# A retention-and-Mish kernel whose first q loads are cut into four pieces, with the order of its opening changed

## The chip, the cores and the metric

The kernel runs on one core of one Trainium2 chip. The metric is the device time of one launch in microseconds (us). A profile of one further execution shows what each engine did: PE (matrix products; PEld is its weight load), DVE (vector), ACT (activation), POOL (GpSimd) and SP, which issues the DMAs.

## The reference

A decaying linear attention is followed by a feed-forward layer with the activation Mish, for 4 batches, 8 heads, 768 positions, head size 64, and an inner width of 2048:

```python
for t in range(S):
    state = gamma * state + outer(k[:, :, t], v[:, :, t])
    y[:, :, t] = scale * einsum(q[:, :, t], state)
x = y.transpose(0, 2, 1, 3).reshape(B * S, H * D)      # 3072 x 512
h = x @ w_in                                           # 512 x 2048
out = (h * tanh(softplus(h))) @ w_out                  # 2048 x 512
```

Everything is float32 in memory; the kernel multiplies in float16.

## The kernel before, in words

**Tiling.** The recurrence is done in chunks of 128 positions. Within a chunk, scores q k^T are masked and multiplied with v; a state of 64 x 64 per head carries what came earlier. The decay is put into the casts: q and k are multiplied with tables of powers of gamma while they are cast from float32 to float16. The 24 chunks form blocks: the first block has four chunks (512 positions, handled as two pairs of chunks), the others two. A block's y, turned so that features lie on the partitions, is `xts[blk]`; `g1` multiplies it with w_in and applies Mish, and the output functions multiply with w_out. Sums of products are saved in places by combining halves (`first_sums`, `weight_sums`: `s1` to `s4`, `t1` to `t4`).

**Order.** It is written by hand: each engine runs its instructions in the order in which the program issues them. All loads go through SP's queue. Load buffers rotate; the float32 stage for q of the first block and for the weights (`wt`, four buffers) is shared.

**The opening** (`first_block`, L1219). SP issues q of the first 512 positions in two halves of four heads (`load_first_q`, L244), then k and v of both pairs in halves of four heads (`load_pair`, L289), 256 KB each; I write k(0,1) for pair 0, second half. Then come the weights (`load_weights`, L1195): w_in in four slices of 512 columns, win0 in four loads, win1 and win2 in two each, by even and odd row blocks, win3 in one, and then slices of w_out. PE fills its waits with `spin` (L454), products of the identity whose results nobody reads.

For each half of q and k there is a cast (`turn_first_q`, L269, and `cast_pair`, L292; on DVE, or POOL where nothing else is said), transposes on PE (`turn_parts`, L253) and a copy from PSUM to SBUF (`taken`, L263; ACT or DVE). Then:

- `pair_scores(n, a)` (L332): 16 products of turned k and q for half a of pair n, and a mask on DVE (L349).
- `cast_pair(n, "v", a)`: v is scaled on ACT (L307).
- `pair_outer` (L356): outer products k^T v, for the state; `pair_state` (L368) adds them up: `mid` on ACT for the first chunk (L373), `suh` and `sth` on DVE (L378, L380), `mid` on DVE for pair 1 (L375).
- `pair_present` (L383): masked scores times v, in two parts; between them PE waits for a copy of one element, `seen` (L1269 on ACT, L1276 on DVE), which shows that the first part is done.
- `pair_past` (L395): the state times q. `pair_xt` (L405) casts the finished y into `xts[0]`.

**Behind the opening.** `open_in` (L671) multiplies `xts[0]` with win0 in an order that follows what is ready (L682). The later units of the first block are `g1(0, u)`, u = 4 to 15, each four products of 128 x 512 with one 128-column part of win1, win2 and win3 (L711) and one Mish on ACT (L720). `first_out` (L756) is the output of the first block; its products are L768. The product of `s3` and `t3` needs L862, a DVE subtraction of parts of wout2 and wout0.

Of the kernel before, what the change touches and what calls it, by code (L numbers as in the profile page):

```python
# [9 lines left out]
FP16 = mybir.dt.float16  # L10
FP32 = mybir.dt.float32
# [5 lines left out]
def kernel(  # L17
# [9 lines left out]
    nc = tc.nc  # L27
# [213 lines left out]

    def load_first_q():  # L244

        qf = wstage.tile([P, H, CPB, D], FP32, name="qfirst", tag="wt", bufs=4)
        for a in range(0, H, H // 2):
            nc.sync.dma_start(
                qf[:, a:a + H // 2],
                q[0, a:a + H // 2, :TB].rearrange("h (p r) d -> p h r d", r=CPB))  # L250
        return qf

    def turn_parts(parts, dst, on_act=False):  # L253
        t_ps = mmps.tile(list(dst.shape), FP16, name="t_ps", tag="mm")
        turn_only(parts, t_ps)
        taken(dst, t_ps, on_act)
# [9 lines left out]
        else:  # L266
            nc.vector.tensor_copy(dst, t_ps)

    def turn_first_q(qf, a, on_act, between=None):  # L269
        n = H // 2  # L270
        q16 = castp.tile([P, 2 * CPB, 2, D], FP16, name="qk16", bufs=4)
        mine = slice(a * n, (a + 1) * n)
        nc.vector.tensor_tensor(  # L273
            in_place(q16), by_head(qf[:, mine]), scale_by_head(qs_four[:, mine]), op=ALU.mult)
        if between is not None:
            between()
        qt = qktp.tile([P, HP // 2, CPB, P], FP16, name="qkt", bufs=6)
        turn_parts(lambda i, r: q16[:, i * CPB + r], qt, on_act)
        first_q.append(qt)

    first_q, pairs = [], {}

    def room_pair(n, names="kv"):
        pairs[n] = {
# [4 lines left out]
    def load_pair(n, nm, a, queue):  # L289
        queue.dma_start(pairs[n][nm][a], pair_src({"q": q, "k": k, "v": v}[nm], n, a))  # L290
# [380 lines left out]
    def open_in():  # L671
# [21 lines left out]
        for f in range(FPS):  # L693
# [3 lines left out]
            if f < 2:  # L697
                nc.scalar.activation(gts[0, f], h[f], AF.Mish, scale=inv_boost3)
        nc.scalar.activation(gtiles[0, 0][:, 2:FPS], two, AF.Mish, scale=inv_boost3)

    def g1(blk, u):
        nt = BLOCKS[blk] * C
# [514 lines left out]
            load_one(g, 2, nc.sync)  # L1217

    def first_block():  # L1219
        qf = load_first_q()  # L1220
        for n in range(2):
            room_pair(n)
        for nm in "kv":
            for n in range(2):
                for a in range(2):
                    load_pair(n, nm, a, nc.sync)
        load_weights()

        pair_at(0, 0)
        spin(46, 1)  # L1230
        turn_first_q(qf, 0, True)
        spin(14, 2)
        turn_first_q(qf, 1, False, lambda: cast_pair(0, "k", 0, vs_two, nc.vector))
        for n, a in ((0, 1), (1, 0), (1, 1)):
            cast_pair(n, "k", a, vs_two)
        nc.gpsimd.memset(tri_half, 0.0)
        for n in range(2):
            nc.gpsimd.affine_select(
                out=tri_half[half(n)], in_=tri_half[half(n)], compare_op=ALU.is_gt, fill=1.0,
                base=0, pattern=[[-1, 2], [-2, D // 2]], channel_multiplier=1)  # L1240
        keep_from(keep_two, 2, [[1, 2], [-1, 2], [-2, D]])
        turn_pair(0, "k", 0, True)
        spin(14)
        pair_scores(0, 0)
        pair_at(0, 1)
        turn_pair(0, "k", 1, True)
        spin(14)
        pair_scores(0, 1)
        turn_pair(1, "k", 0, True)
        cast_pair(0, "v", 0)  # L1250
        turn_pair(1, "k", 1, True)
        cast_pair(0, "v", 1)
        cast_pair(1, "v", 0)
        pair_at(1, 0)
        spin(8)
        pair_scores(1, 0)
        u = [mmps.tile([P, HP, D], FP32, name="u_ps", tag="mm") for _ in range(2)]
        pair_outer(0, u, 0)
        pair_at(1, 1)
        spin(4)  # L1260
        pair_scores(1, 1)
        pair_outer(0, u, 1)
        pair_state(0, u, 0)
        y = [pool.tile([P, 2, 2, C], FP32, name="y_ps", tag=tag)
             for pool, tag in ((mmps, "mm"), (pxps, "px"))]
# [54 lines left out]
        for u in range(NFB):  # L1320
            if u == 0:
                open_in()
            elif u >= FPS:
                g1(0, u)
            if u == 2 * FPS + FPS - 1:
                sums, make = first_sums()
                make[0]()
                make[1]()
                cast_wout(0)
                sum_weights(0, 1)  # L1330
                make[2]()
                cast_wout(1)
                make[3]()
                cast_wout(2)
# [209 lines left out]
```

## Time and profile before

| | |
|---|---|
| median of 3 runs | 191.63 us (191.41 to 191.92) |
| the profiled execution | 191.53 us |
| its span, first to last instruction | 189.7 us |
| PE / DVE / ACT / POOL busy | 97% / 76% / 55% / 39% of the span |
| DMA | 38.82 MB, mean 205 GB/s |

A row of the timeline gives the start in us from the span's start, the time that it covers, the engine, the source line, the operation with what it writes and reads, the shape, the count, and in brackets how long the engine sat idle before it and what ended that. Rows of one kind that follow each other are merged. A product's end is modelled and overlaps the next, so starts are what to compare. DMA rows give the size and the median time from issue to landing. In rows of stages, each engine has its busy time and, in brackets, its count of instructions; the last three columns are the granted PE clock, the share of the 16 DMA engines and the rate.

### The profile page before, as it was taken

To read this page: it belongs to the slowest core of one execution; us is meant where nothing else is said; L and a number is where in the kernel's file an instruction comes from. 1 tells how busy PE (TensorE), PEld (TensorE's weight loads), DVE (VectorE), ACT (ScalarE), POOL (GpSimd) and SP (SyncE) were. 2 spreads that over 40 slices of the span, in tenths; PEclk is the share of its full clock that TensorE was granted. 3 is DMA by queue.
4 is the path that set the end of the run, shared out by engine and by line. 5 is a ranking of instruction groups with operands and counts; after the bars stand their busy time and mean duration, and the time that the engine had idled before them with its cause. 6 is when DMAs were issued, how large, how long until landed. Compare 5 with 4: busy or idle time off the path is not lost.

```text
span 189.7 us, 7650 instructions
## 1 busy us (share of the span) xinstructions
PE 184.5 (97%) x3310; PEld 162.3 (86%) x3310; DVE 144.1 (76%) x297; ACT 105.2 (55%) x199; POOL 73.2 (39%) x101
## 2 busy tenths in 40 slices
PE   7999999999999999999999999999999999999993
PEld 7656478888888888888998998998998998988983
DVE  0788649895977978997898597696698698666862
ACT  3365766264643552553584584583683773873651
POOL 5273000578409746941564624714534800000000
PEclk9999999999999999999999999999999999999999
DMA  5999999999999999999999968992899980301103
GB/s 166 307 314 386 387 384 366 301 315 218 148 249 322 169 235 227 157 276 222 231 211 279 159 143 173 234 206 43 195 198 239 213 162 3 116 3 49 65 3 112
DMA packets 83234, 38.82 MB, mean 205 GB/s; under 512 B 58240, under 2 KB 76288, under 8 KB 83200
## 3 DMA queue, kind: packets, MB, share of 16 engines
q1 hardware_dynamic: 82912, 38.22, 86.3%
q8 instruction: 26, 0.43, 1.1%
q10 hardware_dynamic: 288, 0.11, 0.3%
q14 instruction: 8, 0.07, 0.2%
HBM read 27.31 MB, written 6.29 MB: 177 GB/s over the span
## 4 chain that ended last, share of the span: by engine, by line
PE 94%; DMA 2%; DVE 1%; ACT 1%; issue 0%; DVEq 0%
PE h_ps L923 23%; PE o_ps L1109 23%; PE h_ps L711 17%; PE o_ps L1013 10%; PE o_ps L768 7%; PE y_ps L603 3%; DMA qfirst<-in_q_dram 2%; PE h_ps L682 2%; PE t_ps L261 2%; PE u_ps L497 1%; PE at L489 1%; PE at L460 1%; PE y_ps L390 1%; PE at L341 1%; DVE qk L273 1%; PE u_ps L362 0%
## 5 line engine op out<-in xcount | busy, mean ns | idle before, releaser
L711 PE MATMUL h_ps<-xt,win 128*128 128x256 f16 (+1 forms) x268 | 32.6, 281 | 0.0
L711 PEld LDWEIGHTS <-win 128*128 128x128 f16 x268 | 26.0, 98 | 5.4 <-DVE win L221 0.2
L720 ACT ACTIVATE g<-h_ps 128x512 f16<-128x512 f32 x36 | 21.5, 597 | 14.7 <-PE h_ps L711 14.7
L923 PE MATMUL h_ps<-xt,wsum 128*128 128x128 f16 x448 | 29.6, 219 | 0.0
L935 ACT ACTIVATE g<-h_ps 128x512 f16<-128x512 f32 x42 | 24.3, 598 | 5.6 <-PE h_ps L923 5.6
L923 PEld LDWEIGHTS <-wsum 128*128 128x128 f16 x448 | 26.2, 98 | 0.0
L923 PE MATMUL h_ps<-xt,win 128*128 128x128 f16 x336 | 24.8, 219 | 0.0
L1109 PEld LDWEIGHTS <-gsum 128*128 128x128 f16 x232 | 21.6, 98 | 2.6
L1109 PE MATMUL o_ps<-tmat,gsum 128*128 128x256 f16 (+1 forms) x176 | 21.5, 268 | 0.0
L923 PEld LDWEIGHTS <-win 128*128 128x128 f16 x336 | 20.8, 98 | 0.2
L441 POOL TENSOR_TENSOR v<-vf,qvs 128x512 f16<-128x512 f32 x18 | 18.8, 1055 | 3.4 <-DMA vf<-in_v_dram 3.2
L434 POOL TENSOR_TENSOR qk<-kf,qvs 128x512 f16<-128x512 f32 x18 | 18.9, 1052 | 2.4 <-DMA kf<-in_k_dram 2.4
L431 POOL TENSOR_TENSOR qk<-qf,qvs 128x512 f16<-128x512 f32 x18 | 19.1, 1062 | 1.0 <-PE u_ps L362 1.0
L1109 PEld LDWEIGHTS <-g 128*128 128x128 f16 x184 | 16.5, 98 | 1.6
L971 DVE TENSOR_TENSOR h_ps<-h_ps,hsum 128x512 f32<-128x512 f32 x14 | 9.7, 694 | 9.6 <-PE h_ps L923 9.5
L661 ACT CAST xt<-y_ps 128x512 f16<-128x512 f32 x16 | 10.8, 736 | 10.8 <-PE y_ps L603 10.8
L1450 POOL COPY summed<-gsum 128x1 f16<-128x1 f16 x7 | 1.6, 234 | 36.2 <-DVE gsum L885 29.4
L960 ACT COPY h_ps<-h_ps 128x512 f32<-128x512 f32 x14 | 8.2, 582 | 12.7 <-issue 8.7
L1109 PE MATMUL o_ps<-wout,g 128*128 128x256 f16 (+1 forms) x120 | 14.5, 265 | 0.0
L1119 ACT COPY snap<-o_ps 128x256 f32<-128x256 f32 (+1 forms) x22 | 8.2, 374 | 11.0 <-PE o_ps L1109 11.0
L1132 DVE TENSOR_TENSOR osb<-o_ps,snap 128x256 f32<-128x256 f32 (+1 forms) x22 | 9.1, 414 | 4.2 <-ACT snap L1119 2.8
L948 DVE TENSOR_TENSOR hsum<-h_ps,hsum 128x512 f32<-128x512 f32 x14 | 9.6, 686 | 0.7 <-PE h_ps L923 0.2
(127 smaller groups left out, 338.7 us busy)
## 6 DMA issues: line engine op xcount, KB each, us to landing
out_dram<-osb SPq DMA_DIRECT2D x22, 256.0 KB, 4.0
qf<-in_q_dram SPq DMA_DIRECT2D x18, 256.0 KB, 5.0
kf<-in_k_dram SPq DMA_DIRECT2D x14, 256.0 KB, 5.9
vf<-in_v_dram SPq DMA_DIRECT2D x14, 256.0 KB, 5.5
wt<-in_moe_w_out_dram SPq DMA_DIRECT2D x6, 512.0 KB, 8.7
vf<-in_v_dram SPq DMA_DIRECT2D x20, 128.0 KB, 3.5
wi<-in_moe_w_in_dram SPq DMA_DIRECT2D x4, 512.0 KB, 8.7
kf<-in_k_dram SPq DMA_DIRECT2D x16, 128.0 KB, 4.4
```

Source lines behind the costliest of these rows:

```text
L431: nc.gpsimd.tensor_tensor(in_place(q16.rearrange("p (w x) d -> p w x d", x=2)), by_head(qf), scale_by_head(qs_two[:, heads]), op=ALU.mult)
L434: nc.gpsimd.tensor_tensor(k16.rearrange("p (y w) d -> p w y d", y=2), kf.rearrange("p (w y) d -> p w y d", y=2), boosts.rearrange("p (w y) ...
L441: nc.gpsimd.tensor_tensor(cast[g][2], loaded.pop(g)[2], vs[g % 2].unsqueeze(2).broadcast_to((P, H, D)), op=ALU.mult)
L661: nc.scalar.copy(dst[:, :, x], src)
L711: nc.tensor.matmul(h_ps[:, j, cols], wins[s][f // 2][:, bp, f % 2 * P:(f % 2 + 1) * P], xts[blk][:, bp, cols], start=(bp == 0 and at == 0) ...
L720: nc.scalar.activation(gt, h_ps, AF.Mish, scale=inv_boost3)
L768: nc.tensor.matmul(banks[ij][:, t], x(f)[:, t * P:(t + 1) * P], w(f), start=ij in open_banks, stop=f == fs[-1], skip_group_check=True)
L923: nc.tensor.matmul(o_ps[:, f], w(f // 2, k)[:, f % 2 * P:(f % 2 + 1) * P], x[:, k], start=begin and f == 0 and k == 0, stop=k == 1, skip_g ...
L935: nc.scalar.activation(gt[:, f:f + n, j * C:(j + 1) * C], src, AF.Mish, scale=inv_boost3)
L971: nc.vector.tensor_tensor(pf[p], pa[p], m5[p], op=ALU.add)
L1013: nc.tensor.matmul(o_ps[:, cols], x(f), w(f)[:, cols], start=first and z == 0, stop=z == n - 1, skip_group_check=True)
L1109: nc.tensor.matmul(o_ps[:, c:c + wide], x(f), w(f)[:, c:c + wide], start=first and f == 0 and c == cols.start, stop=f == n - 1, skip_group ...
```

## The change

The first q is loaded, cast and turned in four pieces of two heads (`of_pair`: heads h and h + 2), each 256 KB. SP's order becomes q, q, k(0,0), q, q, k(0,1), k(1,0), k(1,1), and then v as before. DVE casts the four pieces and both halves of k of pair 0; POOL keeps k of pair 1. All copies of turned q and k are made by ACT. The fillers are shared out anew: 38 products before the first turn in place of 46, and shorter runs later. Each turn of k now stands behind the scores of the half before it, the three v casts stand behind the last turn of k, both outer products of pair 0 behind all scores, and those of pair 1 ahead of the present part of pair 1; `seen` on DVE moves behind `mid`. The units 4 and 5 of the feed-forward part are done together in a new function, `next_in`, which takes the even row blocks of w_in for both units ahead of the odd ones.

```diff
+    def of_pair(a, i):
+        h = a * (H // 2) + i
+        return slice(h, h + 3, 2)
+
+    def load_first_q(a, i):
+        if "raw" not in first_q:
+            first_q["raw"] = wstage.tile([P, H, CPB, D], FP32, name="qfirst", tag="wt", bufs=4)
+        nc.sync.dma_start(
+            first_q["raw"][:, of_pair(a, i)],
+            q[0, of_pair(a, i), :TB].rearrange("h (p r) d -> p h r d", r=CPB))
...
+    def cast_first_q(a, i):
...
+        nc.vector.tensor_tensor(
+            in_place(first_q["cast", a][:, i * CPB:(i + 1) * CPB]), first_q["raw"][:, mine],
+            by.unsqueeze(3).broadcast_to((*by.shape, D)), op=ALU.mult)
+
+    def turn_first_q(a, i):
+        if i == 0:
+            first_q[a] = qktp.tile([P, HP // 2, CPB, P], FP16, name="qkt", bufs=6)
+        turn_parts(
+            lambda _, r: first_q["cast", a][:, i * CPB + r], first_q[a][:, i:i + 1], True)
...
+    def next_in():
+        h = [g1_bank(0, FPS + f)[:, 0] for f in range(2)]
+        for bps in ((0, 2), (1, 3)):
+            for f in range(2):
+                for bp in bps:
+                    nc.tensor.matmul(
+                        h[f], wins[1][0][:, bp, f * P:(f + 1) * P], xts[0][:, bp],
+                        start=bp == 0, stop=bp == NBP - 1, skip_group_check=True)
+        for f in range(2):
+            gts[0, FPS + f] = gtiles[0, 0][:, FPS + f]
+            nc.scalar.activation(gts[0, FPS + f], h[f], AF.Mish, scale=inv_boost3)
...
     def first_block():
-        qf = load_first_q()
         for n in range(2):
             room_pair(n)
-        for nm in "kv":
-            for n in range(2):
-                for a in range(2):
-                    load_pair(n, nm, a, nc.sync)
+        for a in range(2):
+            for i in range(2):
+                load_first_q(a, i)
+            load_pair(0, "k", a, nc.sync)
+        for a in range(2):
+            load_pair(1, "k", a, nc.sync)
+        for n in range(2):
+            for a in range(2):
+                load_pair(n, "v", a, nc.sync)
         load_weights()
 
         pair_at(0, 0)
-        spin(46, 1)
-        turn_first_q(qf, 0, True)
-        spin(14, 2)
-        turn_first_q(qf, 1, False, lambda: cast_pair(0, "k", 0, vs_two, nc.vector))
-        for n, a in ((0, 1), (1, 0), (1, 1)):
-            cast_pair(n, "k", a, vs_two)
+        for i in range(2):
+            cast_first_q(0, i)
+        cast_pair(0, "k", 0, vs_two, nc.vector)
+        for i in range(2):
+            cast_first_q(1, i)
+        cast_pair(0, "k", 1, vs_two, nc.vector)
+        for a in range(2):
+            cast_pair(1, "k", a, vs_two)
...
+        spin(38, 1)
+        turn_first_q(0, 0)
+        spin(4, 1)
+        turn_first_q(0, 1)
+        spin(8, 1)
         turn_pair(0, "k", 0, True)
-        spin(14)
+        spin(6, 1)
+        turn_first_q(1, 0)
         pair_scores(0, 0)
         pair_at(0, 1)
+        turn_first_q(1, 1)
+        spin(12)
         turn_pair(0, "k", 1, True)
-        spin(14)
+        spin(12)
         pair_scores(0, 1)
         turn_pair(1, "k", 0, True)
-        cast_pair(0, "v", 0)
-        turn_pair(1, "k", 1, True)
-        cast_pair(0, "v", 1)
-        cast_pair(1, "v", 0)
         pair_at(1, 0)
         spin(8)
         pair_scores(1, 0)
+        turn_pair(1, "k", 1, True)
+        cast_pair(0, "v", 0)
+        cast_pair(0, "v", 1)
+        cast_pair(1, "v", 0)
         u = [mmps.tile([P, HP, D], FP32, name="u_ps", tag="mm") for _ in range(2)]
-        pair_outer(0, u, 0)
         pair_at(1, 1)
         spin(4)
         pair_scores(1, 1)
+        pair_outer(0, u, 0)
         pair_outer(0, u, 1)
         pair_state(0, u, 0)
...
         pair_present(0, y, False)
         aside, u_next = u_banks()
-        spin(6, to=aside)
+        spin(4, to=aside)
...
-        pair_present(1, z, False)
-        nc.vector.tensor_copy(seen, z[1][:, 1, 0, :1])
         u = u_next
         for a in range(2):
             pair_outer(1, u, a)
+        pair_present(1, z, False)
         for m in range(2):
             pair_xt(0, y, m)
         pair_state(1, u, 0)
+        nc.vector.tensor_copy(seen, z[1][:, 1, 0, :1])
         pair_present(1, z, True)
...
         for u in range(NFB):
             if u == 0:
                 open_in()
-            elif u >= FPS:
+            elif u == FPS:
+                next_in()
+            elif u > FPS + 1:
                 g1(0, u)
```

More of the change, by code (lines that the diff above doesn't have):

```diff
@@ L240, in store_due @@
             nc.sync.dma_start(dst, osb)
[L244 to L251, printed above, removed]
+    def of_pair(a, i):
[7 more added lines that the diff above has]
+            q[0, of_pair(a, i), :TB].rearrange("h (p r) d -> p h r d", r=CPB))
     def turn_parts(parts, dst, on_act=False):
@@ L267, in taken @@
             nc.vector.tensor_copy(dst, t_ps)
[L269 to L281, printed above, removed]
+    def cast_first_q(a, i):
+        if i == 0:
+            first_q["cast", a] = castp.tile([P, 2 * CPB, 2, D], FP16, name="qk16", bufs=4)
+        mine = of_pair(a, i)
+        by = qs_four[:, mine]
+        nc.vector.tensor_tensor(
+            in_place(first_q["cast", a][:, i * CPB:(i + 1) * CPB]), first_q["raw"][:, mine],
+            by.unsqueeze(3).broadcast_to((*by.shape, D)), op=ALU.mult)
+    def turn_first_q(a, i):
+        if i == 0:
+            first_q[a] = qktp.tile([P, HP // 2, CPB, P], FP16, name="qkt", bufs=6)
+        turn_parts(
+            lambda _, r: first_q["cast", a][:, i * CPB + r], first_q[a][:, i:i + 1], True)
+    first_q, pairs = {}, {}
     def room_pair(n, names="kv"):
```

## The prediction

> **What bounds the kernel now.** I read the page first, then the waits of the PE, then the PE's rows in the timeline of the opening, then the DMA issues, and last the places later in the span where a weight arrives just before it is used.
>
> ```profile
> span 189.7 us, 7650 instructions
> ...
> PE 184.5 (97%) x3310; PEld 162.3 (86%) x3310; DVE 144.1 (76%) x297; ACT 105.2 (55%) x199; POOL 73.2 (39%) x101
> ```
> ```profile
> PE at L460 <- POOL ident L97: 1.4, 1, 1.4
> PE y_ps L390 <- issue: 0.4, 1, 0.4
> PE t_ps L261 <- DVE qk L273: 0.2, 1, 0.2
> ```
>
> The PE is busy for 184.5 of 189.7 us, and these three waits are all that it has. So time can only be won where PE does filler: the products of L460 (`spin`), which compute nothing and stand in for waits. All of them are in the opening:
>
> ```profile
> 1.36 4.64 PE L460 MATMUL at<-ident 128*128 128x128 f16 x46 [1.36 <-POOL ident L97]
> ...
> 9.33 0.42 PE L341 MATMUL at<-qkt 64*64 64x128 f16 x16
> 9.68 0.40 PE L261 MATMUL t_ps<-ident,qk 128*128 128x128 f16 x4
> ...
> 10.77 0.42 PE L341 MATMUL at<-qkt 64*64 64x128 f16 x16
> ...
> 12.19 0.42 PE L341 MATMUL at<-qkt 64*64 64x128 f16 x16
> 12.71 0.32 PE L362 MATMUL u_ps<-v,qk 64*64 64x64 f16 x16
> ...
> 13.29 0.42 PE L341 MATMUL at<-qkt 64*64 64x128 f16 x16
> ...
> 15.42 0.25 PE L390 MATMUL y_ps<-am,v 64*64 64x128 f16 x3 [0.38 <-issue]
> ...
> 16.32 0.42 PE L390 MATMUL y_ps<-wsum,v 64*64 64x128 f16 x16
> ...
> 17.05 3.65 PE L682 MATMUL h_ps<-xt,win 128*128 128x256 f16 x24
> ```
>
> From 17.05 us on PE has real work without a gap. The first question is when L682 starts in the changed kernel. The second is whether an earlier start survives, because the weights arrive at a pace of their own:
>
> ```profile
> 20.84 0.10 PEld L711 LDWEIGHTS <-win 128*128 128x128 f16 x1 [0.21 <-DVE win L221]
> ```
> ```profile
> 33.18 1.50 DVE L233 CAST wout<-wt 128x1024 f16<-128x1024 f32 x2
> ...
> 35.32 1.53 DVE L862 TENSOR_TENSOR tmat<-wout,wout 128x1024 f16<-128x1024 f16 x1
> ```
> ```profile
> 36.97 0.10 PEld L768 LDWEIGHTS <-wsum 128*128 128x128 f16 x1
> ```
> ```profile
> wt<-in_moe_w_out_dram SPq DMA_DIRECT2D x1, 512.0 KB, 9.7
> ```
> ```profile
> 15.50:34.00 18.50, 18.43 (x219) 13.71 (x219) 13.56 (x27) 12.00 (x20) 1.83 (x3) 1.00 1.06 377
> ```
>
> The weight load at 20.84 is the one that waits for win1's odd rows: its engine already sat idle for 0.21 us. The load at 36.97 is that of the product of `s3` and `t3`, and `t3` is written by L862, which ends at 35.32 + 1.53 = 36.85. L862 stands behind the last cast of wout2, whose 512 KB took 9.7 us from issue to landing. That is waiting in the queue, since the 16 DMA engines are full from 15.5 to 34 us (share 1.06, 377 GB/s). The bytes ahead of wout2 are the same in the changed kernel, so it lands when it does now. **PE has about 0.1 us in hand there (36.97 against 36.85); whatever more the opening saves is waited off at that load.**
>
> **The change part by part.**
>
> *The loads.* Two q loads of 512 KB become four of 256 KB, and k(0,0) goes between them. The bytes ahead of k(0,1) stay 1 MB of q and 256 KB of k, so its landing stays.
>
> ```profile
> qfirst<-in_q_dram SPq DMA_DIRECT2D x1, 512.0 KB, 5.1
> ```
> ```profile
> 8.34 3.04 POOL L311 TENSOR_TENSOR qk<-kf,qvs 128x512 f16<-128x512 f32 x3 [4.68 <-DMA kf<-in_k_dram]
> ```
> ```profile
> 4.93 1.23 DVE L273 TENSOR_TENSOR qk<-qfirst,qvs 128x1024 f16<-128x1024 f32 x1 [4.07 <-DMA qfirst<-in_q_dram]
> 6.36 1.23 DVE L273 TENSOR_TENSOR qk<-qfirst,qvs 128x1024 f16<-128x1024 f32 x1 [0.20 <-DMA qfirst<-in_q_dram]
> 7.50 0.69 DVE L311 TENSOR_TENSOR qk<-kf,qvs 128x512 f16<-128x512 f32 x1
> ...
> 12.66 2.35 DVE L349 TENSOR_TENSOR wsum<-at,keep_four 128x1024 f16<-128x1024 f32 x2 [0.20 <-PE at L341]
> 14.94 0.42 DVE L378 TENSOR_TENSOR suh<-u_ps,mid 128x256 f32<-128x256 f32 x1
> ...
> 16.33 0.42 DVE L375 TENSOR_TENSOR mid<-u_ps,sth 128x256 f16<-128x256 f32 x1
> ```
>
> The q halves land at about 4.8 and 6.3, 1.5 us per 512 KB, so the quarters should land near 4.1, 4.8, 6.5 and 7.2 (estimate), k(0,0) between them at 5.7 in place of 7.3, and k(0,1) at 8.2 as now (POOL's wait ends at 8.34). Two more issues on SP cost nothing, as the queue holds work throughout (the second q half is issued 5.1 us before it lands); if that cover failed, each would cost its issue, about 0.5 us.
>
> By the Trainium skill, page "DMA: Bandwidth & Descriptors", section "Rules for kernel authors", the split is the wrong way: it asks for 1 MiB and more per transfer, as each has a fixed cost of some 2.0 us. The trace differs as far as it goes: the second half lands 1.5 us behind the first, less than its bytes and 2 us of its own would take. Taken as serial it would be a rival, priced below.
>
> *The casts.* Four DVE casts of 0.69 take the place of two of 1.23, and k(0,1) moves from POOL (1.0 each by the row of three) to DVE. DVE waits for landings, so the first k cast ends at 6.4 and that of k(0,1) at 8.2 + 0.7 = 8.9. POOL's two remaining casts end at 11.3 as today, for k(1,1) lands at 10.
>
> *PE up to the last scores.* The last q quarter is cast at 8.0. PE turns it at 8.0, runs three fillers and has reached k(0,1) at 8.9. Now this turn is at 9.68, so 0.78 is gained. From a turn to its scores it is 10.77 - 9.68 = 1.09 (transposes, ACT's copy, the handovers), and scores take 9.68 - 9.33 = 0.35. In the new order each turn of k follows the scores before it, so the chain is serial: turn 8.91, scores 10.00, turn 10.35, scores 11.43 (now 12.19), turn 11.78, scores 12.87 (now 13.29). The gain shrinks from 0.76 to 0.42, since today the two turns of the second pair stand side by side.
>
> *ACT, where the rest goes.* The casts of v now stand behind all copies of k.
>
> ```profile
> 12.03 0.63 ACT L307 ACTIVATE v<-vf 128x512 f16<-128x512 f32 x1
> 12.56 0.58 ACT L265 COPY qkt<-t_ps 128x512 f16<-128x512 f16 x1
> 13.03 1.16 ACT L307 ACTIVATE v<-vf 128x512 f16<-128x512 f32 x2
> 14.08 0.37 ACT L373 CAST mid<-u_ps 128x256 f16<-128x256 f32 x1
> ...
> 14.39 0.65 ACT L307 ACTIVATE v<-vf 128x512 f16<-128x512 f32 x1
> ```
>
> The last k copy begins at 11.78 + 0.44 = 12.22 (now 12.56), and then three casts of v run where two did: one follows the other after 0.53 (two in 13.03 to 14.08). So v begins at 12.7, `mid` at 12.7 + 3 x 0.53 = 14.3 (now 14.08) and the fourth v at 14.65 (now 14.39): a loss of 0.25. The outer products of the first chunk, which waited for v at 12.71, come at 13.4.
>
> *The end of the opening.* `mid` ends at 14.7, so DVE starts `suh` at 14.75 (now 14.94, behind its last mask; masks take 1.2 by the row of two, and the last one, 0.45 behind the scores' start at 12.87, would end at 14.55). The state follows, two operations of 0.42 with their handovers, and the next `mid` (L375) from 15.8 (now 16.33): 0.55 gained, most of it from PE's hold at 15.42, which I expect to be gone (below). DVE's one-element copy `seen`, moved behind it, ends near 16.28, as now, and lets L390 go at 16.32, as now. But the last products of L400 no longer wait for `mid` (16.76 now), which saves 0.15. **Sum: L682 starts at 16.9 in place of 17.05, a gain of 0.15, uncertain by 0.3 either way over some 25 handovers.**
>
> *`next_in`.* It does the even rows of two products ahead of the odd ones, and asks for win1's odd rows 0.43 us later (two products of 128x512). This takes away the wait seen at 20.84, and costs nothing, as ACT's first result is late by 0.43 on an engine with idle time. Bounds: 0 and 0.2. It is needed for any gain above 0.1, and that gain then meets the load at 36.97.
>
> So of 0.15 about 0.1 is left. The profiled execution took 191.53 us (span 189.7), 0.1 below the median of 191.63. The forecast is 191.53 - 0.1 = 191.43, and by the median 191.5: no change that the measurement can tell (0.3%, 0.57 us).
>
> **The rivals.**
>
> *Slower: PE's instructions come late.* PE stood from 15.03 to 15.42 with nothing to wait for but its own program ("issue"), in the middle of one group of L390. Shortly before, 16 KB of instructions came on a queue of their own:
>
> ```profile
> q8 instruction: 1, 0.02, 6.0%
> ```
>
> This is from the DMA answer for 12.7 to 13.9 us. If the fetch starts at a place that PE passes at about 9.7 now, it comes 0.8 earlier and the hold is gone, as I took it. If it starts where PE stands as it begins (the outer products, 12.71), these come 0.68 later in the new order; the hold ends at 16.1, and from there the new order needs 1.57 (rest of L390 and L400 0.15, outer products 0.26, L390 0.45 to its result, `seen` 0.25, L390 and L400 0.46). L682 starts at 17.67, 0.62 late: 192.25. It decides from 15.1 us, where PE reaches that place. Chance 0.18.
>
> *Slower: half clock for longer.*
>
> ```profile
> 1.35:5.37 4.02, 4.01 (x38) 4.02 (x39) 1.00 0.84 253
> 5.37:6.00 0.63, 0.62 (x11) 0.45 (x8) 1.00 1.13 334
> ```
>
> These count filler: one per 0.107 us up to 5.37, then one per 0.056. The change cuts the first run to just 38, so that real work begins at 5.4. If PE idled there and stayed slow, its work up to the turn of k(0,1), some 3 of the 3.5 us by the groups above, would take twice as long; 0.6 of waits absorb a part: 2.4 late, 194. Against it: q's first quarter is ready at 4.9, so there is no idle time. Chance 0.02. The Trainium skill, page "TensorE: Matmul & The Clock Gate", Part 1, puts the step at one busy window of some 3.4 us that runs free of the kernel's start; the step here, 4.0 us behind PE's first product, agrees.
>
> *Slower: the split loads do not overlap.* The second half took 5.1 us to land of which 1.5 is its bytes; with 2.6 of start-up for each of two added loads k(0,1) and all behind it are 5 us late: 196.6. Chance 0.02.
>
> *Faster: the queue fills sooner.*
>
> ```profile
> DMA packets 24, 0.02 MB, mean 51 GB/s; under 512 B 5, under 2 KB 24, under 8 KB 24
> ```
> ```profile
> DMA packets 144, 0.15 MB, mean 369 GB/s; under 512 B 0, under 2 KB 144, under 8 KB 144
> ```
>
> These are 2.4 to 2.8 and 3.0 to 3.4 us: the stream begins, all but stops, and is full from 3. If the shorter first load closes this hole, every landing comes 0.45 earlier, the opening gains 0.15 + 0.45 and the cap at 36.97 moves along: 191.0. Against it: nothing shows that the hole is due to size. With it goes that ACT's order costs less than I think. Chance 0.25.
>
> *Nothing as said:* the quarters land no sooner than the halves. The chain starts at k(0,1), so the time is the forecast's.
>
> **How the numbers follow.** Forecast 0.53 (191.2 to 191.8), faster 0.25, slower 0.22. The range takes in the 191.0 and the 192.25 and leaves out the two dear cases: 190.8 to 192.3. Faster by over 0.3%: 0.26 (the faster case and 0.01 of the forecast's edge); within: 0.52; slower: 0.22.
>
> **What would show it.** Right: k(0,1) turned near 8.9, three scores near 10.0, 11.4 and 12.9, v cast on ACT from 12.7, `open_in`'s first product at 16.9, no "issue" wait in the opening, and a short wait of PE's weight load near 36.97 for L862. Wrong: landings of q and k that are not at 4.1 to 8.2, a hold at 15 to 16, an L862 that ends before 36.8, or `open_in` starting under 16.5 or over 17.4.

## The result, and the profile after

| | before | changed |
|---|---|---|
| median | 191.71 us (191.33 to 192.84, 22 runs) | 192.9 us (191.59 to 194.75, 22 runs) |
| profiled execution (span) | 191.53 us (189.7) | 192.99 us (191.1) |

The changed kernel is slower: ratio 1.0058, 95% interval 1.0042 to 1.0074, 1.2 us by the medians. Two of its runs (194.62 and 194.75 us) count as slow and are left out of the ratio. Its runs also scatter over 3 us. The profiled execution lost 1.46 us, so it has a little more of the loss than the median run.

The page of the changed kernel, its span, the busy time of its engines and its chain by engines:

```profile
span 191.1 us, 7656 instructions
...
PE 183.7 (96%) x3310; PEld 161.3 (84%) x3310; DVE 144.7 (76%) x299; ACT 106.6 (56%) x202; POOL 72.6 (38%) x100
...
PE 78%; DMA 13%; SPq 4%; DVE 2%; issue 0%; ACT 0%
```

PE does no more work than before (it is busy 0.8 us less), but the chain that ended last now runs through DMA for 13% of the span. What PE waits for, in us in total, times and longest:

```profile
PE at L465 <- POOL ident L97: 1.4, 1, 1.4
PE t_ps L263 <- DVE qk L316: 1.1, 1, 1.1
PE at L346 <- ACT qkt L267: 0.7, 2, 0.5
PE y_ps L395 <- DVE seen L1313: 0.4, 1, 0.4
PE o_ps L785 <- DVE tmat L879: 0.3, 1, 0.3
```

The hold on its own instructions is gone. In its place stand a wait for the first cast of k, and one for the sum that feeds the product of `s3` and `t3` (here L785 and L879; L768 and L862 before). The reason for the first is in DVE's rows of the opening:

```profile
6.44 0.69 DVE L316 TENSOR_TENSOR qk<-kf,qvs 128x512 f16<-128x512 f32 x1 [1.33 <-DMA kf<-in_k_dram]
7.17 1.47 DVE L276 TENSOR_TENSOR qk<-qfirst,qvs 128x512 f16<-128x512 f32 x2
8.85 0.69 DVE L316 TENSOR_TENSOR qk<-kf,qvs 128x512 f16<-128x512 f32 x1 [0.21 <-DMA kf<-in_k_dram]
```

DVE waits for k(0,0) until 6.44, and k(0,1) comes at 8.8. By issue and landing in the trace, the first two quarters of q land at 3.64 and 4.39, earlier than forecast (4.1 and 4.8); then k(0,0) takes until 6.42, the other quarters until 7.14 and 7.92, and k(0,1) until 8.82 (8.16 before). The rate of the stream shows where the time went. In stages (the last three columns are PE's granted clock, the share of the DMA engines and GB/s), first before, then changed:

```profile
2.50:2.90 0.40, 0.40 (x6) 0.40 (x5) 0.00 (x0) 0.15 (x1) 0.31 (x4) 1.00 0.23 33
3.80:5.20 1.40, 1.40 (x16) 1.40 (x15) 0.27 (x1) 0.00 (x0) 0.00 (x0) 1.00 1.09 382
```
```profile
2.50:2.90 0.40, 0.40 (x6) 0.40 (x5) 0.00 (x0) 0.14 (x1) 0.31 (x4) 1.00 0.93 328
3.80:5.20 1.40, 1.40 (x24) 1.40 (x23) 1.30 (x2) 0.00 (x0) 0.00 (x0) 1.00 0.78 173
```

The start-up hole (33 GB/s) is closed, and a longer one has opened at 3.8 to 5.2 us: 173 GB/s where 382 ran. SP had issued four more loads by 3.8 us, so it is not for want of issued loads. I call it the hole below. What follows on PE:

```profile
9.60 0.40 PE L263 MATMUL t_ps<-ident,qk 128*128 128x128 f16 x4
...
10.67 0.42 PE L346 MATMUL at<-qkt 64*64 64x128 f16 x16
...
12.09 0.42 PE L346 MATMUL at<-qkt 64*64 64x128 f16 x16 [0.24 <-ACT qkt L267]
...
13.51 0.42 PE L346 MATMUL at<-qkt 64*64 64x128 f16 x16 [0.46 <-ACT qkt L267]
...
16.96 0.42 PE L395 MATMUL y_ps<-wsum,v 64*64 64x128 f16 x16 [0.43 <-DVE seen L1313]
...
17.53 0.72 PE L687 MATMUL h_ps<-xt,win 128*128 128x256 f16 x5
```

`open_in` starts at 17.53, 0.48 late. Two more losses come behind it, both where a weight is late. DVE's casts of win2, its sums with the last cast of wout2, and PE's loads of what they make:

```profile
23.30 0.76 DVE L221 CAST win<-wi 128x512 f16<-128x512 f32 x2 [1.93 <-DMA wi<-in_moe_w_in_dram]
24.66 0.76 DVE L221 CAST win<-wi 128x512 f16<-128x512 f32 x2 [0.60 <-DMA wi<-in_moe_w_in_dram]
```
```profile
25.14 0.87 PEld L728 LDWEIGHTS <-win 128*128 128x128 f16 x7 [0.57 <-DVE win L221]
```
```profile
35.57 0.69 DVE L233 CAST wout<-wt 128x1024 f16<-128x1024 f32 x1 [0.56 <-DMA wt<-in_moe_w_out_dram]
36.30 0.69 DVE L878 TENSOR_TENSOR tmat<-wout,tmat 128x1024 f16<-128x1024 f16 x1
36.91 1.53 DVE L879 TENSOR_TENSOR tmat<-wout,wout 128x1024 f16<-128x1024 f16 x1
```
```profile
38.49 0.77 PEld L785 LDWEIGHTS <-wsum 128*128 128x128 f16 x8 [0.55 <-DVE tmat L879]
```

The last load of wout2 lands at 35.55 in place of 33.96, and the weight load that was at 36.97 is at 38.49. Following one and the same ACT instruction through both traces gives the account of this execution: +0.48 behind the opening and still behind `next_in`, +0.74 behind win2, +1.43 behind `t3`, and from there it stays within 0.02 to the end. So 0.48 of the loss comes from the opening and 0.95 from the two late weights.

### The profile page after: what moved, and what is told of

It reads as the page before. It is cut to its first block, busy times and chain, and to the rows that moved or that the text cites. A ratio compares the mean times of both kernels' runs of the same rounds, so it can differ in the third digit from the quotient of the medians.

```text
span 191.1 us, 7656 instructions
## 1 busy us (share of the span) xinstructions
PE 183.7 (96%) x3310; PEld 161.3 (84%) x3310; DVE 144.7 (76%) x299; ACT 106.6 (56%) x202; POOL 72.6 (38%) x100
## 4 chain that ended last, share of the span: by engine, by line
PE 78%; DMA 13%; SPq 4%; DVE 2%; issue 0%; ACT 0%
PE h_ps L940 23%; PE o_ps L1126 23%; PE h_ps L728 11%; PE o_ps L1030 10%; DMA wt<-in_moe_w_out_dram 5%; DMA wi<-in_moe_w_in_dram 5%; PE o_ps L785 4%; DMA vf<-in_v_dram 3%; PE y_ps L608 3%; SPq L295 3%; PE at L494 1%; PE u_ps L502 1%; SPq L251 1%; DVE tmat L879 1%; PE t_ps L263 0%
## 5 line engine op out<-in xcount | busy, mean ns | idle before, releaser
L728 PE MATMUL h_ps<-xt,win 128*128 128x256 f16 (+1 forms) x260 | 31.0, 278 | 0.1
L728 PEld LDWEIGHTS <-win 128*128 128x128 f16 x260 | 25.1, 98 | 4.8 <-DVE win L221 0.6
L737 ACT ACTIVATE g<-h_ps 128x512 f16<-128x512 f32 x34 | 20.3, 597 | 14.7 <-PE h_ps L728 14.7
L952 ACT ACTIVATE g<-h_ps 128x512 f16<-128x512 f32 x42 | 24.2, 597 | 5.5 <-PE h_ps L940 5.4
L940 PEld LDWEIGHTS <-win 128*128 128x128 f16 x336 | 20.8, 98 | 0.2
```

What stands on the lines that cost most here:

```text
L728: nc.tensor.matmul(h_ps[:, j, cols], wins[s][f // 2][:, bp, f % 2 * P:(f % 2 + 1) * P], xts[blk][:, bp, cols], start=(bp == 0 and at == 0) ...
L737: nc.scalar.activation(gt, h_ps, AF.Mish, scale=inv_boost3)
L940: nc.tensor.matmul(o_ps[:, f], w(f // 2, k)[:, f % 2 * P:(f % 2 + 1) * P], x[:, k], start=begin and f == 0 and k == 0, stop=k == 1, skip_g ...
L952: nc.scalar.activation(gt[:, f:f + n, j * C:(j + 1) * C], src, AF.Mish, scale=inv_boost3)
```

## The experiments

Landings and starts in us from the profiled execution; "of before" means that only what the edit says is changed.

| run | median (range, runs) | ratio to before, 95% | k(0,1) lands | `open_in` | wout2 lands |
|---|---|---|---|---|---|
| e1, new order, old loads | 192.45 (192.09 to 193.48, 12) | 1.0035 (1.0018, 1.0052) | 8.09 | 17.09 | 33.81 |
| e2, of before: quarters | 192.17 (191.85 to 193.65, 12) | 1.0033 (1.0011, 1.0056) | 9.55 | 18.33 | 34.97 |
| e3, changed, wider fillers | 193.4 (192.35 to 194.33, 7) | 1.0072 (1.0045, 1.01) | 8.62 | 18.50 | 34.05 |
| e4, changed, q in halves | 192.82 (192.65 to 193.1, 6) | 1.005 (1.0037, 1.0064) | 8.13 | 17.85 | 33.90 |
| e5, changed, half then quarters | 192.04 (191.41 to 195.25, 12) | 1.0014 (0.999, 1.0037) | 8.18 | 17.18 | 33.83 |
| e6, of before: opening held | 193.16 (192.33 to 193.68, 6) | 1.0077 (1.0051, 1.0103) | 8.05 | 17.65 | 33.86 |
| e7, of before: `next_in` | 191.88 (191.14 to 192.95, 12) | 1.0018 (0.9997, 1.0038) | 8.22 | 16.92 | 33.83 |
| e8, changed, once more | 194.42 (1) | | 8.97 | 17.89 | 36.43 |
| e9, of before: quarter, then rest | 195.57 (194.98 to 197.41, 6) | 1.0225 (1.0192, 1.0258) | 7.98 | 19.88 | 33.77 |
| e10, e5 with a trimmed opening | 191.57 (191.16 to 194.42, 12) | 1.0003 (0.9988, 1.0018) | 8.15 | 16.85 | 33.80 |
| e11, e10 with POOL held | 191.98 (191.32 to 194.43, 12) | 1.0012 (0.9989, 1.0036) | 8.22 | 17.06 | 33.95 |
| e12, e2 once more | 192.11 (1) | | 8.95 | 17.77 | 34.78 |

**e1: the new order on the old loads.** q in two halves ahead of all k, as before; the casts, the turns and the fillers follow the landings, the rest is the changed kernel.

```diff
...
         for a in range(2):
-            for i in range(2):
-                load_first_q(a, i)
+            load_first_q(a, 0)
+        for a in range(2):
             load_pair(0, "k", a, nc.sync)
...
```

> The loads of before (two q halves, then k, then v) under the changed order of scores, v casts and outer products; next_in kept; q is cast and turned ahead of k. Theory A (the loads are at fault: k(0,0) and all behind it came 0.66 us late, and the weights 1.6): k(0,1) lands at 8.2 as before, open_in starts at 16.9 to 17.0, wout2 lands near 34, time 191.4 to 191.7. Rival B (the new order of the opening is at fault by itself): open_in at 17.5 and over 192.5.

No hole, the old landings, `open_in` at 17.09 and `t3` not waited for: until 110 us the execution stands 0.04 behind that of before. Yet it is 0.7 us slower, a time that neither theory gave, and the trace has that in two places far behind, 0.33 near 120 us, where PE stood for its own instructions (its weight load was idle for 0.43), and 0.55 near 141 us. The second, DVE and then POOL:

```profile
140.15 0.42 DVE L894 TENSOR_TENSOR gsum<-gsum,g 128x512 f16<-128x512 f16 x1
140.49 1.26 DVE L893 TENSOR_TENSOR gsum<-g 128x512 f16<-128x512 f16 x1
```
```profile
140.18 1.29 POOL L446 TENSOR_TENSOR v<-vf,qvs 128x512 f16<-128x512 f32 x1 [1.68 <-PE h_ps L940]
```

A sum that took 0.42 in the kernel before takes 1.26 beside a cast on POOL. So the order by itself does not lengthen the opening, and most of its cost in this execution came from a meeting of DVE and POOL over 120 us later. Whether most executions of e1 have it there isn't shown.

**e2 and e12: the quarters alone.** The kernel before, its q in four loads of 256 KB in the place of two.

```diff
-            nc.sync.dma_start(
-                qf[:, a:a + H // 2],
-                q[0, a:a + H // 2, :TB].rearrange("h (p r) d -> p h r d", r=CPB))
+            for i in range(2):
+                mine = slice(a + i, a + i + 3, 2)
+                nc.sync.dma_start(
+                    qf[:, mine], q[0, mine, :TB].rearrange("h (p r) d -> p h r d", r=CPB))
```

> The kernel before, with its two q loads cut into four of 256 KB in the same place; no k between them, order, casts and fillers of before. Theory A1 (cutting q is what delays the stream): k(0,1) lands at 8.8 and wout2 over 35, time 192.5 or more. Theory A2 (k standing between the q pieces, or the earlier fetch of instructions, does it): landings as before or up to 0.4 sooner, time 191.5 to 191.8.

> The kernel before with q in four quarters and nothing else changed, one more look, because its profiled execution (193.65) was the slowest of its twelve (median 192.17). Theory A (the hole is there every time but its depth varies, and the median run has a shallow one): a hole from 3.7 us again, the last quarter between 6.9 and 7.6, k(0,1) between 8.6 and 9.3, open_in at 17.3 to 18.0, time 191.9 to 192.6. Rival B (the hole is always as deep): the last quarter at 7.7, k(0,1) at 9.5, open_in at 18.3, 193 or more. Rival C (most executions have no hole): the last quarter at 6.3 and k(0,1) at 8.1.

Stages of e2, then of e12:

```profile
3.80:5.20 1.40, 1.40 (x22) 1.40 (x21) 0.81 (x1) 0.00 (x0) 0.00 (x0) 1.00 0.66 173
```
```profile
3.80:5.20 1.40, 1.40 (x16) 1.40 (x15) 0.38 (x1) 0.00 (x0) 0.00 (x0) 1.00 0.95 303
```

The hole comes with the four loads alone, without k between them and without the new order. Its depth varies: 173 GB/s in the slowest of the runs, k(0,1) at 9.55 and 193.65 us; 303 GB/s in the execution of e12, k(0,1) at 8.95 and 192.11 us. That is theory A of e12. Theory A1 of e2 is right on the landings, but the median of 192.17 stays under its 192.5. The varying depth may be one reason for the wide scatter of the changed kernel; it isn't the only one, for e8 below has a shallower hole than the first execution of that kernel and a longer time.

**e3: an instruction fetch moved.** The first fillers as 19 products that are two columns of 128 wide, in place of 38 of one: the same time on PE with fewer instructions.

```diff
-        spin(38, 1)
+        spin(38, 2)
```

> The changed kernel with its first 38 fillers of 128 columns made 19 of 256: the same time on PE and 38 instructions fewer, so the first fetch of PE's instructions, which follows PE's place in its program, comes about 1.3 us later (12.7 in place of 11.4, behind the v loads). Theory A3 (the fetch in the midst of the v loads delays them, SP then issues wi2 late, and the next fetch delays the weights again): v(1,0) lands near 13.3 in place of 14.4, wout2 lands at 34.2 to 34.4, time 192.0 to 192.2. If the fetch has no part in it: 192.7 to 193 as the changed kernel.

The fetch of PE's next 16 KB moved from 11.37 us to 14.46, so it no longer fell among the loads of v, and wout2 landed at 34.05, as theory A3 said. The hole is there (230 GB/s at 3.8 to 5.2). The time is not A3's, for now PE itself needs the block:

```profile
15.72 0.26 PE L367 MATMUL u_ps<-v,qk 64*64 64x64 f16 x8
16.95 0.38 PE L367 MATMUL u_ps<-v,qk 64*64 64x64 f16 x24 [0.97 <-issue]
```

PE stands 0.97 us with nothing to wait for but its own program, and `open_in` is at 18.50. An earlier landing of the weights is worth nothing to a kernel whose opening ends a microsecond later.

**e4: k between halves.** The changed kernel with q in two loads of 512 KB, k(0,0) between them, k(0,1) behind the second.

```diff
+        mine = slice(a * (H // 2), (a + 1) * (H // 2))
...
-            for i in range(2):
-                load_first_q(a, i)
+            load_first_q(a, 0)
```

> The changed kernel with q in two loads of 512 KB, k(0,0) between them and k(0,1) behind the second. If the place of k makes the hole that held k(0,0) back to 6.4 us: the hole stays, k(0,1) lands at 8.8, open_in near 17.6, time 192.5 to 193. If the cutting of q makes it: k(0,0) at 5.8, k(0,1) at 8.2, open_in near 17.0.

There is no hole (353 GB/s), the landings are as good as those of before (k(0,0) 5.70, k(0,1) 8.13, wout2 33.90), and the kernel is still slower by 0.5%. Two things make the opening late. The second half of q comes whole at 7.24, so its turns and the fillers behind them reach k(0,1) at 9.57. And then DVE meets POOL:

```profile
15.28 0.42 DVE L383 TENSOR_TENSOR suh<-u_ps,mid 128x256 f32<-128x256 f32 x1
15.81 0.82 DVE L385 TENSOR_TENSOR sth<-suh,gch 128x256 f16<-128x256 f32 x1
```
```profile
15.74 1.36 POOL L221 CAST win<-wi 128x512 f16<-128x512 f32 x2 [2.48 <-DMA wi<-in_moe_w_in_dram]
```

`sth` takes 0.82 where it takes 0.43 in the kernel before, because it came 0.07 behind POOL's cast of win0 and not 0.28 ahead of it.

**e5: the first half whole.** The changed kernel; only the first two quarters are one load again.

```diff
+        if (a, i) == (0, 1):
+            return
+        mine = of_pair(a, i) if a else slice(0, H // 2)
         nc.sync.dma_start(
-            first_q["raw"][:, of_pair(a, i)],
-            q[0, of_pair(a, i), :TB].rearrange("h (p r) d -> p h r d", r=CPB))
+            first_q["raw"][:, mine], q[0, mine, :TB].rearrange("h (p r) d -> p h r d", r=CPB))
```

> The changed kernel with the first half of q in one load of 512 KB, k(0,0) behind it, the second half still in two quarters, then k(0,1). Theory A (the two small loads at the head of the queue cause the hole in the stream, and everything on PE follows from the landings): first half at 4.8, k(0,0) 5.7, quarters 6.5 and 7.2, k(0,1) 8.1 to 8.2, the landings that the prediction had for this part; the turn of k(0,1) near 9.0, open_in at 16.9 to 17.1, time 191.7 to 192.0. Rival B (any quarter opens a hole, wherever it stands): the quarters at 7.0 or later, k(0,1) at 8.8, open_in near 17.5, time 192.5 to 193. Rival C (the order on PE is what costs): landings as in A, but open_in at 17.4 or later.

```profile
3.80:5.20 1.40, 1.38 (x17) 1.20 (x15) 0.23 (x1) 0.00 (x0) 0.00 (x0) 1.00 1.14 353
```

The hole is gone; landings at 4.87, 5.76, 6.51, 7.31 and 8.18, as forecast for these pieces. The turn of k(0,1) at 9.29, `open_in` at 17.18 and the median are a little past A's bounds; the span is 189.7 as before, and the interval takes in 1. One load more in front is all that stands between this kernel and the changed one, 1.0014 and 1.0058, and the two intervals do not meet.

**e6: a late opening by itself.** The kernel before with 0.86 us of filler ahead of `open_in`.

```diff
+        spin(16, to=h[0].rearrange("p (i c) -> p i c", c=P).unsqueeze(1))
         for pair in range(2):
             for bp in (0, 2):
```

> The kernel before with four filler products of 512 columns (0.86 us) ahead of open_in and nothing else changed, all loads as before. Theory A (a late opening is paid twice: DVE's sums of wout2 slip with PE into the time in which POOL casts the next q, the two engines hold each other up, and the product of s3 and t3 waits): open_in's first product at 17.9, one of the two sums ahead of t3 takes 1.4 in place of 0.69, the product of s3 and t3 is 1.1 to 1.3 late, time 192.8 to 193.0. Rival B (the delay is paid once): 0.86 late throughout, time 192.5 to 192.6. Rival C (slack behind the opening takes it up): under 192.2.

In this execution PE stood only 0.2 for its own instructions, where it stood 0.38 before, so `open_in` is 0.60 late. At `t3` 0.37 more is lost, in the way that theory A said. DVE's sums (L862 and L863 here) and POOL's casts of the next q:

```profile
35.09 1.43 DVE L862 TENSOR_TENSOR tmat<-wout,tmat 128x1024 f16<-128x1024 f16 x1
36.44 1.52 DVE L863 TENSOR_TENSOR tmat<-wout,wout 128x1024 f16<-128x1024 f16 x1
```
```profile
34.93 2.49 POOL L311 TENSOR_TENSOR qk<-qf,qvs 128x512 f16<-128x512 f32 x2 [16.55 <-DMA qf<-in_q_dram]
```

Before, the first of these sums begins 0.29 ahead of POOL's first cast and takes 0.69, and only the second takes 1.53. Here the first begins 0.16 behind that cast, and both take long. A late opening is thus paid for a second time. This execution (192.33) is the fastest of the six; the median lost 0.8 us more, and where isn't shown.

**e7: `next_in` alone** in the kernel before, called in place of `g1(0, 4)` and `g1(0, 5)` as in the diff of the change.

> The kernel before with next_in in place of the units 4 and 5, nothing else. Theory A (next_in costs nothing and there is no wait left for it to take away but the 0.2 of the weight load): within 0.2 of the kernel before, 191.5 to 191.9. Rival B (next_in, or the shifts of a few hundredths that it brings to DVE against POOL, carries the 0.7 that the new order with the old loads showed): 192.2 to 192.5.

Theory A: 191.88, an interval that takes in 1, and no wait of PE for win1.

**e8: the changed kernel again.**

> The changed kernel once more, one look. Theory A (the hole behind the first two quarters is a property of the load order): no hole at 2.5 to 2.9, a hole from about 3.7, q's last quarter at 7.7 to 7.9, k(0,1) at 8.6 to 8.9, open_in at 17.4 to 17.6. Theory B (the late second half of w_in's third slice, 1.35 us behind its place, was a chance meeting of an instruction fetch with the load queue): the last load of wout2 lands at 34.0 or at 35.5, not necessarily as in the first look. Rival (both come with the load order): 35.5 again.

The hole (222 GB/s at 3.8 to 5.2) and the late landings are there again, k(0,1) at 8.97, and win2 even later:

```profile
24.25 0.77 DVE L221 CAST win<-wi 128x512 f16<-128x512 f32 x2 [2.13 <-DMA wi<-in_moe_w_in_dram]
```

Theory A holds for the hole, with landings up to 0.2 past its bounds; `open_in` at 17.89 is later than its bound, since `sth` met POOL here too (0.67). wout2 landed at 36.43, later than in the first execution, which speaks for the rival and against a chance meeting.

**e9: one small load in front.** The kernel before with q as 256 KB and 768 KB.

```diff
-        for a in range(0, H, H // 2):
+        for mine in (slice(0, 2), slice(2, H)):
             nc.sync.dma_start(
...
+                qf[:, mine], q[0, mine, :TB].rearrange("h (p r) d -> p h r d", r=CPB))
```

> The kernel before with q loaded as 256 KB (two heads) and then 768 KB (six heads), nothing else changed. Theory A (what fails at the head of the queue is the third load: its packets do not flow at the full rate before about 5 us, so the two loads in front must hold 5 us of work): no hole, first piece at 3.5, the rest at 6.3, k(0,0) at 7.2, k(0,1) 8.1, open_in at 17.0 to 17.1, time 191.5 to 192.0. Rival B (the size of the first load does it): a hole behind the first 256 KB, the rest of q at 6.9 or later, k(0,1) at 8.7 or later, open_in at 17.6 or later, time 192.2 or more.

The landings are theory A's: 3.61, 6.17, 7.07 and 7.98, with 361 GB/s at 3.8 to 5.2. A single small load in front does the stream little harm (271 GB/s at 3.0 to 3.7); the loads that run at half rate are those behind two of them. The time is not A's, by a mistake of mine: the first cast needs four heads, so it now waits for 6.17, and PE stands for 2.1 us. Behind that idle time PE ran at half clock to 11 us in the profiled execution:

```profile
PE t_ps L260 <- DVE qk L272: 2.1, 1, 2.1
```
```profile
7.50:11.00 3.50, 3.42 (x27) 2.99 (x28) 2.73 (x4) 1.01 (x1) 2.85 (x3) 0.54 1.17 290
```

Its mean granted clock over the span is 0.991. Four of the six runs have 0.998 to 1.000 and take 194.98 to 195.79 us all the same, so the half clock is not the main part of the loss.

**e10: the opening trimmed.** e5 with fewer fillers ahead of the turn of k(0,1), and `seen` back ahead of `mid`.

```diff
         turn_first_q(1, 1)
-        spin(12)
+        spin(4)
         turn_pair(0, "k", 1, True)
...
+        pair_present(1, z, False)
+        nc.vector.tensor_copy(seen, z[1][:, 1, 0, :1])
         u = u_next
         for a in range(2):
             pair_outer(1, u, a)
-        pair_present(1, z, False)
...
-        nc.vector.tensor_copy(seen, z[1][:, 1, 0, :1])
```

> The order of the changed kernel on the loads of one half and two quarters, with 8 fewer filler columns of 128 ahead of the turn of k(0,1), and the present part of pair 1 with its one-element copy put back ahead of the outer products and of mid. Theory A (my cap: an earlier opening is waited off at the product of s3 and t3, and at k behind it): turn of k(0,1) at 8.95, scores at 10.0, 11.4, 12.9, open_in at 16.5, the product of s3 and t3 waits 0.3 to 0.4 and starts at 36.7 to 36.9, as in the kernel before or 0.2 earlier; time 191.4 to 191.7. Rival B (no cap): the whole 0.5 stays, 191.1. Rival C (the chain is held somewhere else in the opening): open_in at 16.9 or later.

The turn (8.93) and the scores (10.00, 11.42, 12.84) came as expected, `open_in` only at 16.85, near rival C's bound. From the last scores it takes 4.01 us with `seen` ahead of `mid` and took 3.98 with it behind (e5), so that place is worth nothing. The 0.20 gained stays through `t3` without a wait, and the measurement shows no difference from before.

**e11: POOL held.** e10 with `cast_qk` behind the sum `t3`, and one element of `t3` read by POOL first.

```diff
-        cast_qk()
         plain(0, 0, 1)
         plain(0, 1, 1)
         weight(0, 2)
+        cast_qk()
...
         def cast_qk():
+            nc.gpsimd.tensor_copy(summed, tmats[1][:, 0, FPS - 1, d_model // 2 - 1:])
```

> The kernel of the run before with POOL's casts of the next q made to wait until DVE's sum t3 is written, so that the two engines do not stand in each other's way at 35 us. Theory A: the second sum takes 0.69 in place of 1.53 and ends at 36.0, POOL casts at 36.1 and 37.1, the product of s3 and t3 starts without a wait at 36.4 to 36.5, and the next wait is that for the turn of q or k near 38 us; of the 0.5 of the opening 0.2 to 0.4 stays; time 191.3 to 191.5. Rival B (the sum's 1.53 us are its own and not POOL's doing): it keeps 1.53 and the time is that of the run before. Rival C (POOL's delay is paid at the turns of q): slower than the run before by 0.3 or more.

```profile
34.70 0.69 DVE L880 TENSOR_TENSOR tmat<-wout,tmat 128x1024 f16<-128x1024 f16 x1
35.31 0.68 DVE L881 TENSOR_TENSOR tmat<-wout,wout 128x1024 f16<-128x1024 f16 x1
```
```profile
36.20 2.04 POOL L318 TENSOR_TENSOR qk<-qf,qvs 128x512 f16<-128x512 f32 x2
```

The sum takes 0.68 and not 1.53, and POOL's pair of casts 2.04 and not 2.71 as in e10: the mechanism of theory A is shown, rival B is out. Its time isn't reached: nothing waited at this place in e10, and this execution fell behind e10's in other places, by 0.21 in the opening, 0.12 at the turns near 38 us, 0.32 near 73 us and 0.67 near 120 us, where PE stood 0.49 for its own instructions. By the medians e11 is 0.4 slower than e10, which is rival C's bound; but the intervals overlap, and the turns that rival C names cost 0.12 here. Neither e10 nor e11 beats the kernel before.

## Why the prediction was wrong, step by step

**The landings: the step that failed.** "The bytes ahead of k(0,1) stay 1 MB of q and 256 KB of k, so its landing stays." It took the stream for one whose rate doesn't depend on how the bytes are cut. k(0,1) landed 0.66 late, behind the hole. e2 shows that the cut alone makes the hole, e4 and e5 that with 512 KB in front there is none, and e9 that one small load in front doesn't make it. I had seen the start-up hole of the old loads and priced its closing as the faster rival (191.0). It did close, and a microsecond later the stream fell to half its rate; that possibility I had not thought of. `open_in` came at 17.53 where 16.9 was forecast: by e5's 17.18, some 0.35 of the 0.63 is the hole, and 0.28 the start of PE's chain (below).

**Issues on SP cost nothing:** right as far as the issues go (about 0.5 us each, as before). But the reason given, that the queue holds work throughout, doesn't keep the rate up: in the hole four more loads stood issued, and the stream ran at 173 GB/s.

**PE from the landings on.** The spacing of 1.43 from score to score is right (10.67, 12.09, 13.51), and so is the way from the last scores to `open_in`: 4.03 forecast, 4.02 measured. The start was too early by itself: e5, with the forecast's landings, turns k(0,1) at 9.29, not 8.91. I let PE turn the last quarter of q when it is cast, at 8.0, but the scores of k(0,0) stand ahead of that turn in the program, and they wait for ACT's copies of q, q and k(0,0), three of 0.59 between 6.15 and 8.01. So that turn is at 8.41. By e5, without the hole the opening would have ended at 17.18, a loss of 0.13 and not a gain of 0.15.

**The hold at 15.42:** right, it is gone; the fetch came at 11.37 in place of 12.75. The rival that priced it higher didn't come in the changed kernel, but e3 shows that it exists (0.97 us). The half-clock rival didn't come: PE stood for 1.1 us in the opening, and its products kept the full rate behind that. Nor did the serial loads, for k(0,1) is 0.66 late and not 5. Their price had a slip: 5.1 less 1.5 is 3.6, and the 2.6 that it used is the first half's 4.1 less 1.5.

**`next_in`:** right, no gain or loss that can be measured (e7).

**The cap at `t3`.** "The bytes ahead of wout2 are the same in the changed kernel, so it lands when it does now." The same premise in another place, and a larger part of the loss: wout2 landed 1.59 late. Only 0.24 of that is there at win1, whose last half lands at 20.58 in place of 20.34; the rest arises between win1 and win2, and its cause is open (below). That PE would wait there was right, but not for the reason given: it waits since the weights are late, not since the opening is early. With old landings an opening 0.20 earlier meets no wait there (e10).

**The price of lateness,** a term that the sum did not have. It counted what an early opening saves and stopped at 0.1. A late one costs its own 0.5 to 0.9 us and more: DVE's sums slip behind POOL's casts (e6, 0.37), `sth` behind that of win0 (e4, 0.4), and win2 and wout2 come late on their own (0.26 and 0.69 in the changed kernel).

The Trainium skill, page "DMA: Bandwidth & Descriptors", section "Rules for kernel authors", spoke against the split, and the direction of the result is the one that it gives. The fixed cost of some 2.0 us, which the same page states in its section "Anatomy of one DMA — SWDGE (gpsimd) path", is not seen as a cost of each load: two loads more cost k(0,1) 0.66 us, in the hole, and the quarters of e5 land 0.75 to 0.80 apart.

**What stays open.** Three things.

- Why the loads behind two small ones run at half rate and those behind one do not. The runs fit another reading as well, the one of theory A in e9: what stands behind the first two loads doesn't flow at the full rate before about 5 us. With quarters in front the first two loads hold 512 KB, in e4 and e5 768 KB, before and in e9 1 MB. No run separates the number of small loads from the bytes ahead.
- Why win2 and all behind it slip. The executions of e2, e8, e12 and the changed kernel, all with quarters in front, have 2.0 to 2.9 us between the last half of win1 and the first half of win2, both of 512 KB, where the others have 1.3 to 1.4. So the slip begins with win2's first half, not with its second as the expectation of e8 has it. An instruction fetch lies at that place, but it does in e3 too, which has 1.34. The stream is slow before it: from 16 to 19 us it ran at 242 GB/s in e8, 341 in the changed kernel, 363 in e2 and 378 in e12, and the gaps shrink in the same order (2.89, 2.69, 2.27, 2.01). In the kernel before and in e3 it ran at 387, and in none of the others under 382. What slows it isn't shown.
- What the new order costs by itself in the median run. e1 has the old landings and 1.0035, e5 nearly the forecast's and 1.0014, e4 has no hole and 1.005. So e5 against the changed kernel shows that the two small loads in front make most of the loss, but it doesn't show that the order is free.

## What to carry to other kernels

The first loads of a kernel are a stage of their own: while the queue starts up, cutting them finer brings the first piece sooner (3.6 in place of 4.8 us) and may starve the pieces behind it, so look at the rate over the first five microseconds and not at the bytes. When a stage becomes late, don't stop at its own delay: look for pairs of DVE and POOL instructions that just miss each other now, and for weights that come just in time. And when a chain is timed, walk each engine's program in order; the instruction ahead in the queue counts, not only the data.

## What the runs showed of the hardware

- DVE and POOL hold each other up: a sum of two SBUF operands takes 0.69 alone and 1.43 to 1.53 beside POOL's casts, and POOL's pair 2.04 alone and 2.75 beside it. The Trainium skill, page "SBUF — State Buffer", section "Who interferes with whom", says that a DVE instruction with two SBUF inputs contends with a GpSimd instruction that reads SBUF; the trace agrees, and e11 shows it by taking the meeting away.
- PE's instructions come in blocks of 16 KB through the same DMA engines, and PE stood 0.38 (before), 0.97 (e3) and 0.49 us (e11) with nothing else to wait for. That it stood for a block is inferred from the times: in each of the seven such holds of 0.15 us or more in these traces, PE went on 1.2 to 1.5 us behind the end of a block's packet. The Trainium skill, page "Runtime: NRT & Kernel Launch", section "Instruction fetch mechanics", calls such a crossing mostly hidden; most are here, these are not. The loads feel it too: in 13 of the 14 traces the load that landed next behind the first of these packets came 0.8 to 1.4 us later than the spacing of its neighbours (before, 2.03 us behind the load ahead of it, with 0.67 between the next ones).
- PE's step from half to full rate is not at a fixed time. The spacing of its products falls from 0.107 to 0.056 us at 4.2 us in the changed kernel, at 5.4 before and at 7.1 in e3 (the column of the clock says 1.00 on both sides of it). In e8 four transposes at 5.39 us take 0.63, and 0.39 at 7.47. In e9 PE had stepped up at 4.3; behind an idle time of 2.1 us from 5.5 it ran at half clock from 7.8 to 11.2. A like idle time from 7.1 in e2 was not followed by that.
